# Six inner products in the second matrix product of block 0, with a new home for one set of sums, a shorter layer norm on GpSimd and a remade order table

## The chip, the cores and the metric

The kernel runs on one core of a Trainium2 chip. The metric is the device time of one execution in microseconds. The kernel before takes 338.49 us in the median of three runs (338.16 to 338.64).

In the profile, PE is TensorE's matmuls, PEld its weight loads, DVE is VectorE, ACT is ScalarE, POOL is GpSimd, and SP is SyncE, which issues nearly all transfers (SPq is its sequencer). L868 is line 868 of the kernel's file.

## The reference

```python
def reference(x, w1, b1, w2, b2):      # x (1, 2048, 1024), w1 (1024, 3584), w2 (3584, 1024), all bfloat16
    y = _layernorm(x, axis=-1)         # eps 1e-5
    h = _gelu(jnp.einsum("bsd,df->bsf", y, w1) + b1)
    return jnp.einsum("bsf,fd->bsd", h, w2) + b2
```

## The kernel before

The 2048 rows are worked on in two blocks of 1024. In each block h = gelu(y w1 + b1) comes first, then h w2. Both matrix products use seven products of half-sized operands in place of eight (a Strassen-like scheme). The operands of most of these are sums of quarters of h and w2, made by VectorE, and their results are added up by VectorE and ScalarE.

In the second matrix product, one of the seven products can itself be done by the same scheme. A *plain* product is 4 x 14 matmuls of 512 columns. An *inner* product is 7 half-size products of 14 matmuls of 256 columns, which is an eighth fewer columns, and costs more sums and additions. Which products are inner is a table, with one entry for each block:

```python
SEQ2 = (1, 5, 2, 6, 7, 3, 4)             # the order of the seven products
INNER = ((1, 5, 2, 3, 4), SEQ2)          # block 0: five of them inner; block 1: all seven
```

Block 0 stores its sums of w2 in DRAM, so that block 1 can load them.

All work is a list of operations with dependencies. A planner with estimated durations gives each engine one fixed program, guided by a table of hand-tuned shifts (`ORDER`, some 120 entries). Every engine then gets its program in that order, and an instruction that has to wait holds up all behind it (in a trace below ScalarE stands 5.45 us so, with copies for TensorE behind).

```python
    def _emit(eng, name, ops, sems):   # one engine's program
        for o in ops:
            wait(o.deps)               # semaphores of what it depends on
            inst = o.fn(eng)
            inst.then_inc(sems[o.sem], o.inc)
```

While block 0's second product runs, the rows of block 1 are loaded into eight "x tiles" of 128 rows, normalised, and sent to their transposed place by transposing transfers. The last steps of the layer norm of one tile are:

```python
    vp = add("POOL", 0.2, ... tensor_scalar(out=vpe, in0=sum_of_squares, scalar1=1/D, scalar2=LN_EPS, mult, add))
    rs = add("POOL", 0.6, ... tensor_tensor(out=rstd, in0=vpe, in1=nhalf, op=ALU.pow))      # 1/sqrt
    nb = add("POOL", 0.3, ... tensor_tensor(out=bias, in0=mean, in1=rstd, op=ALU.mult))
    y  = add("ACT", 1.3, ... activation(out=x16, in_=x_sb, func=Identity, scale=rstd, bias=bias))
```

Block 0's product 7 is plain, and product 3 is inner, with its sums of w2 kept in the place of two used w1 tiles (`Y0`):

```python
    M7 = plain(7, S3, B[7], hb, False, [(o,) for o in O12])
    ...                                  # 4 output additions on VectorE, 4 copies O3 on ScalarE
    sub3 = inner(3, S4, inner_sums(3, B[3], Y0, war_of(sub2, 2), True), X0, war_of(sub2), O=..., out=12)
```

Of the kernel before, what the change touches and what calls it, by code (L numbers as in the profile page):

```python
# [23 lines left out]
P = 128  # L24
# [8 lines left out]
INNER = ((1, 5, 2, 3, 4), SEQ2)  # L33
# [6 lines left out]
    G1_5g_0_5:5.5 G1_5g_1_5:8.8 G2_5g_0_3:-15.8 G2_5g_1_3:0.8 G3_5g_0_3:7.3 G3_5g_0_5:-4.7 G3_5g_1_1:-25.3  # L40
    G4_5g_1_1:13 G6_5g_0_5:-21 G7_5g_0_3:9.2 G7_5g_0_5:6.5 M11_1:8.3 M15_0:17 M24_0:-3.1 M27_1:5.7 M43_0:-8.5
    M47_0:7.7 M51_1:7.2 M57_0:16.8 M6_0_0:3.3 M72_1:-20.2 O12_0_1:11.2 O12_0_3:8.4 P1_0_6:10.3 P1_0_9:-1.1
    P1_1_2:-2.7 P1_1_3:-18.7 P1_1_6:0.2 P2_0_12:-1 P2_0_5:0.7 P3_0_10:-9.9 P3_0_11:5.1 P3_0_12:-7.3 P3_0_2:-10.3
    P3_1_6:9.8 P4_0_3:7.4 P4_0_9:-17.7 P4_1_0:40.5 P4_1_1:54.4 P4_1_3:2 P6_0_12:-3.6 P6_0_4:1.1 P6_1_11:4.1
    P7_0_6:-33.7 c7_0_11:2.3 c7_0_5:1.2 c7_0_8:-5.5 c7_0_9:8.4 c7_1_12:9.1 c7_1_13:1.2 g12_1_1:13.1 g12_1_3:2.2
    g21_1_8:25.8 g22_0_2:1.3 g22_0_3:1.6 gS0_5g_1_3:20 gS1_5g_0_3:-6.6 gS1_5g_0_5:11.2 gS3_5g_0_5:14.9 g_0_3_2:-14.6
    hS2_0_1:-7.5 hS3_1_0:8.3 hS4_0_1:-4.8 hS4_0_3:39 iS3_1_1_0:41 iS3_2_0_0:8.3 iS5_3_1_0:28.6 iS5_4_0_0:-14.1
    iS5_5_0_0:-10 iS6_5_0_0:-3.7 iT4_1_0_0:4.1 iT4_2_0_0:3.8 iT4_3_0_0:13.3 iT5_3_0_0:14.2 iT6_1_0_0:4.6
    iT6_2_0_0:1.3 iT6_4_0_0:6.6 iT6_5_0_0:-8.9 k5_3_1:16.7 k5_5g_0_5:35.6 o12_3_0:-17 pT1_2:-34.8 pT1_3:15 pT1_6:4.8
    pT2_1:1.7 pT2_2:7.7 pT3_3:10.8 pT3_5:-2.2 pT4_0:-7.2 pT4_3:-4.3 pT4_4:-7 pT4_5:-2.4 pT4_6:7.9 plain_0_7_2None:35  # L50
    plain_0_7_3None:8.5 pw2_0:-4.4 r11_5g_1_5:-18.2 r12_5_0:10.8 r22_1_0:14.3 r22_5g_0_3:33.7 s2_2_0:-7.2
    sd1_0_2:11.5 sn1_0_9:12.1 sn1_1_10:2.8 sn1_1_5:-0.5 sn5_0_4:-29.1 st0_5_0:-3.9 w1T13_1_0:3.4 w1T1_0_4:30.1
    w1T1_0_6:-5.1 w1T1_1_2:3.5 w1T2_1_1:26.1 w1T3_0_6:-17.7 w1T4_1_3:15 w1_0_0_1:9.9 w1_0_3_0:-7.9 w1_0_5_0:-24
    w1_0_5_1:-0.6 w1_1_0_0:0.7 w1_1_6_1:-1.9 w6_0_11:-4.1 w6_0_5:-9.5 w6_1_5:-44.2 wi5_3:20.8 x0_0_1:-11.2 x1_0:4.8
    y1_6:-8.5 yS1_1_0:6.2 yS2_0_0:8.2 yS2_1_0:-3.4 yS4_1_0:8.6 yi13_1:14.5 yi2_0:-15 yt0_6_0:-2.3
# [5 lines left out]
LAT = 0.12  # L61
PE_LAT = 0.2
# [43 lines left out]
class Planner:  # L106
# [42 lines left out]
    def place(self):  # L149
# [12 lines left out]
        while left:  # L162
# [35 lines left out]
            free[e] = r + c  # L198
# [60 lines left out]
def bass_standalone__mixer_channel_mlp__prompt_kernel(  # L259
# [24 lines left out]
    with ExitStack() as es:  # L284
# [20 lines left out]
        nhalf = sb("nhalf", [P, 1], F32)  # L305
        st_sb = sb("st_sb", [P, NT, 12], F32)
# [75 lines left out]
        c_nh = add("POOL", 0.1, lambda e: e.memset(nhalf[:, :], -0.5), (), -8, "nhalf")  # L382

# [14 lines left out]
        def warm(n, deps, prio):  # L398
# [8 lines left out]
                                                    identity=identb[0:FT, 0:FT]), ())], (c_idb, b1_ld), 11.0, "b1t",  # L407
# [56 lines left out]
        def ln_act2(s, i, prio, war=None):  # L464
# [14 lines left out]
            if junk is junk1:  # L479
                for u in (NU - 2, NU - 1):  # L480
                    h_head.setdefault((22, u), []).append(a2)
            vp = add("POOL", 0.2, lambda e: e.tensor_scalar(out=vpe_sb[:, i:i + 1], in0=st_sb[:, i, 0:1],
                                                           scalar1=1.0 / D, scalar2=LN_EPS, op0=ALU.mult, op1=ALU.add),
                     (a2,), prio + 0.003, f"vpe{s}_{i}")
            rs = add("POOL", 0.6, lambda e: e.tensor_tensor(out=rstd_sb[:, i:i + 1], in0=vpe_sb[:, i:i + 1],
                                                            in1=nhalf[:, :], op=ALU.pow), (vp, c_nh), prio + 0.004,
                     f"rstd{s}_{i}")
            nb = add("POOL", 0.3, lambda e: e.tensor_tensor(out=st_sb[:, i, 1:2], in0=mv_sb[:, i, 1:2],  # L488
                                                            in1=rstd_sb[:, i:i + 1], op=ALU.mult), (rs, a1), prio + 0.005,
                     f"nb{s}_{i}")  # L490
# [82 lines left out]

        def w1_t1(s, c, prio):
            n = s * NC + c
            T1_of[(s, c)] = add("DVE", 0.65, lambda e: e.tensor_tensor(
                out=t1_sb[:, n % 2, 0].rearrange("p k (v c) -> p k v c", v=2), in0=w1raw(n, 0, 1), in1=w1raw(n, 0, 0),
                op=ALU.subtract), [w1_ld[(s, c)][0], *t1_use.get(n - 2, {}).get(1, ())], prio, f"w1T1_{s}_{c}")

        def w1_sums(s, c, prio):  # L580
# [3 lines left out]
            war = t1_use.get(n - 2, {})  # L584

            def tt(k, x0, x1, deps):
                return add("DVE", 0.65, lambda e: e.tensor_tensor(out=tv(k), in0=x0, in1=x1, op=ALU.subtract),  # L587
                           [*deps, *war.get(k, ())], prio + 0.5 * k, f"w1T{k}_{s}_{c}")

            if n > 1 and (s, c) not in GROUPED:  # L590
# [4 lines left out]
                    [*ld, *war.get(1, ()), *war.get(3, ())], prio + 0.5, f"w1T13_{s}_{c}")  # L595
# [5 lines left out]
            w1_use[n] = list(dict.fromkeys((T1, T2, T3, T4)))  # L601
            return {1: T1, 2: T2, 3: T3, 4: T4}
# [3 lines left out]
        def mm1_plain(c, prio):  # L606
# [3 lines left out]
            for b in range(2):  # L610
                hold = [Holder(banks) for _ in range(4)]
                done = {f: [] for f in range(4)}
                for i in range(b * TH, (b + 1) * TH):
                    t = i % TH
                    y = y_in[(0, i)]
                    for j, f in ([(j, f) for j in range(2) for f in range(4)] if i == 0 else
# [7 lines left out]
                        o = add("PE", len(ks) * MM128, fn, list(dict.fromkeys([*done[f][:1]] + [d for _, dd in fn for d in dd])),  # L624
# [244 lines left out]
        x_gate = {}  # L869
        PU = 2  # L870
# [58 lines left out]
        def mm2_block(s, W):  # L929
# [10 lines left out]
            last_ = {}  # L940
            done = lambda p: users[p]
# [94 lines left out]
            def inner(p, a, Yo, xb, war, O=None, bias=None, out=None, gate=(), ogate=(), kk=None, tmp=None, tail=False):  # L1036
# [21 lines left out]
                subs, ev = {}, {}  # L1058

# [284 lines left out]
            for m in (n - 1, n):  # L1344
                w1_use[m] = w1_use[m] + done(3) + kept[3]
# [167 lines left out]
```

## Time and profile before

| | kernel before |
|---|---|
| time, median of 3 | 338.49 us |
| profiled execution | 337.93 us, span 336.2 us |
| TensorE busy | 98% of the span |
| VectorE busy | 84%; 135 to 195 us: 54.6 of 60 us |
| ScalarE, GpSimd busy | 52%, 7% |
| waits of TensorE after its first 8 us | none |

The prediction below shows the lines.

### The profile page before, as it was taken

What the parts mean: (1) busy time and instruction counts of PE and PEld (TensorE: products, weight loads), DVE (VectorE), ACT (ScalarE), POOL (GpSimd) and SP (SyncE); (2) the same over time, 40 slices, a digit from 0 to 9 for tenths busy, and PEclk for the clock granted to TensorE, in tenths of its full rate; (3) what the DMA queues carried; (4) which work ended last, traced back from release to release, by engine and by line L of the source; (5) the groups of instructions that cost most, each with busy time, mean ns of one, the idle gap of its engine ahead of it and who ended that gap; (6) DMA issues with size and microseconds to landing.
All of it is one profiled execution on the core that took longest, in us unless ns stands there. A gap on an engine that the chain in (4) does not pass through costs nothing.

```text
span 336.2 us, 6035 instructions
## 1 busy us (share of the span) xinstructions
PE 329.3 (98%) x2399; PEld 223.3 (66%) x2399; DVE 281.3 (84%) x381; ACT 173.2 (52%) x292; POOL 22.5 (7%) x47
## 2 busy tenths in 40 slices
PE   4999999999999999999999999999999999999996
PEld 4977445445468885547875555544545888888885
DVE  3896789998999999979999888886738879999984
ACT  5675978566786687612113666765676521010200
POOL 2420120000020413200000000000000000000000
PEclk9899999999999999999999999999999999999999
DMA  7896999797868999899859549839971999999103
GB/s 269 257 181 182 355 354 321 247 329 262 279 238 305 353 336 361 227 318 379 320 173 328 181 174 336 288 138 292 351 226 50 386 319 367 333 326 311 65 2 125
DMA packets 80310, 89.47 MB, mean 266 GB/s; under 512 B 15130, under 2 KB 67226, under 8 KB 79770
## 3 DMA queue, kind: packets, MB, share of 16 engines
q1 hardware_dynamic: 80138, 88.95, 81.6%
q8 instruction: 19, 0.31, 0.4%
q10 hardware_dynamic: 144, 0.13, 0.1%
q14 instruction: 9, 0.07, 0.1%
HBM read 61.81 MB, written 24.38 MB: 256 GB/s over the span
## 4 chain that ended last, share of the span: by engine, by line
PE 93%; ACT 3%; POOL 1%; DVE 1%; DMA 1%; issue 0%
PE ps L767 42%; PE ps L1063 34%; PE ps L978 7%; PE ps L619 5%; PE ps L692 5%; DMA x_sb<-in_x_dram 1%; POOL st_sb L488 1%; PE ps L504 1%; ACT t_sb L474 1%; ACT t_sb L469 1%; PE ps L1068 0%; ACT sn_sb L962 0%; ACT ps L962 0%; DVE st_sb L418 0%; ACT x_sb L491 0%
## 5 line engine op out<-in xcount | busy, mean ns | idle before, releaser
L767 PE MATMUL ps<-yw_sb,t_sb 128*128 128x512 f16 x336 | 80.0, 379 | 0.0
L767 PE MATMUL ps<-yw_sb,w_sb 128*128 128x512 f16 x312 | 74.7, 379 | 0.0
L792 ACT ACTIVATE h_sb<-ps,b_sb 128x512 f16<-128x512 f32 x78 | 52.9, 686 | 37.0 <-PE ps L767 32.3
L767 PEld LDWEIGHTS ps<-yw_sb,t_sb 128*128 128x128 f16 x336 | 32.8, 98 | 35.8 <-DVE ps L807 0.2
L767 PEld LDWEIGHTS ps<-yw_sb,w_sb 128*128 128x128 bf16 x312 | 30.3, 98 | 33.2 <-ACT ps L780 0.3
L854 DVE TENSOR_TENSOR h_sb<-h_sb 128x2048 f16<-128x2048 f16 (+2 forms) x36 | 38.6, 1084 | 7.3 <-ACT h_sb L792 5.3
L962 ACT COPY sn_sb<-ps 128x512 f32<-128x512 f32 x27 | 15.5, 583 | 32.9 <-DVE o_sb L942 18.2
L1063 PE MATMUL ps<-w2a_sb,h_sb 128*128 128x256 f16 (+1 forms) x252 | 30.3, 273 | 0.0
L942 DVE TENSOR_TENSOR sn_sb<-ps,sn_sb 128x512 f32<-128x512 f32 x35 | 24.0, 687 | 5.3 <-PE ps L1063 4.6
L1063 PEld LDWEIGHTS ps<-w2a_sb,h_sb 128*128 128x128 f16 x252 | 24.7, 98 | 3.9
L942 DVE TENSOR_TENSOR o_sb<-ps,sn_sb 128x512 bf16<-128x512 f32 (+1 forms) x29 | 19.3, 670 | 6.3 <-PE ps L1063 3.7
L978 PE MATMUL ps<-w2a_sb,h_sb 128*128 128x512 f16 x112 | 24.5, 379 | 0.0
L1063 PE MATMUL ps<-w_sb,t_sb 128*128 128x256 f16 x196 | 23.4, 273 | 0.1
L962 ACT COPY ps<-sn_sb 128x512 f32<-128x512 f32 x12 | 7.1, 589 | 30.3 <-PE ps L1063 24.6
L780 ACT COPY ps<-ps 128x512 f32<-128x512 f32 x26 | 14.9, 577 | 14.6 <-PE ps L767 14.5
L1063 PEld LDWEIGHTS ps<-w_sb,t_sb 128*128 128x128 f16 x196 | 19.0, 98 | 2.7 <-ACT sn_sb L962 0.4
L807 DVE TENSOR_TENSOR ps<-ps,sn_sb 128x512 f32<-128x512 f32 x26 | 17.6, 694 | 3.4 <-PE ps L767 3.3
L792 ACT ACTIVATE h_sb<-sn_sb,b_sb 128x512 f16<-128x512 f32 x26 | 18.5, 717 | 3.7 <-DVE sn_sb L821 2.8
L587 DVE TENSOR_TENSOR t_sb<-w_sb,t_sb 128x1024 f16<-128x1024 bf16 x26 | 17.9, 687 | 2.8 <-PE ps L767 1.6
L978 PEld LDWEIGHTS ps<-w2a_sb,h_sb 128*128 128x128 f16 x112 | 11.0, 98 | 12.8
L821 DVE TENSOR_TENSOR sn_sb<-ps,sn_sb 128x512 f32<-128x512 f32 x20 | 13.6, 686 | 5.1 <-PE ps L767 5.0
L619 PE MATMUL ps<-yw_sb,w_sb 128*128 128x128 f16 x256 | 16.7, 226 | 0.4 <-DVE yw_sb L511 0.4
(125 smaller groups left out, 485.4 us busy)
## 6 DMA issues: line engine op xcount, KB each, us to landing
w_sb<-in_w_dram SPq DMA_DIRECT2D x28, 512.0 KB, 5.6
x_sb<-in_w_dram SPq DMA_DIRECT2D x21, 256.0 KB, 6.0
w_sums<-x_sb SPq DMA_DIRECT2D x21, 256.0 KB, 3.5
w2a_sb<-w_inner_sums SPq DMA_DIRECT2D x12, 448.0 KB, 7.3
x_sb<-in_x_dram SPq DMA_DIRECT2D x15, 256.0 KB, 4.3
w_inner_sums<-w_sb SPq DMA_DIRECT2D x4, 896.0 KB, 8.2
x_sb<-w_sums SPq DMA_DIRECT2D x2, 1792.0 KB, 9.1
w_sb<-w_inner_sums SPq DMA_DIRECT2D x8, 448.0 KB, 6.9
```

The lines of the kernel that those rows point to most:

```text
L587: return add("DVE", 0.65, lambda e: e.tensor_tensor(out=tv(k), in0=x0, in1=x1, op=ALU.subtract), [*deps, *war.get(k, ())], prio + 0.5 * k, ...
L619: fn = [(lambda e, b=b, hb=hold[f], f=f, k=k, t=t: e.matmul(ps[:, hb.k, t * P:(t + 1) * P], lhsT=lhs[:, k, f * P:(f + 1) * P], rhs=yop[f"A ...
L692: fn = [(lambda e, k=k, v=v: e.matmul(ps[:, bank[r].k, v * QN:(v + 1) * QN], lhsT=xo()[:, k, v * P:(v + 1) * P], rhs=yv()[:, k, :], start= ...
L767: fn = [(lambda e, k=k: e.matmul(ps[:, hold[p].k, :], lhsT=lhs[:, k, :], rhs=yop[yo][:, k, :], start=(first and k == 0), stop=(k == KH - 1 ...
L780: return e.copy(out=dst, in_=src) if o_.eng == "ACT" else e.tensor_copy(dst, src)
L792: r = h_ok[(s, q, u)] = add("ACT", 0.70, lambda e: e.activation(out=dst, in_=src(), func=ACT.Gelu_apprx_tanh, bias=b1_sb[:, f:f + 1], scal ...
L807: o2 = add("DVE", 0.7, lambda e: e.tensor_tensor(out=b5v(b5), in0=b5v(b0), in1=v5(), op=ALU.add), (P6, *o5), pt[7] - SLOT, f"w6_{nm}", all ...
L854: o = add("DVE", cost2(w * dst.shape[-1]), lambda e, k0=k0, k1=k1: e.tensor_tensor(out=dst[:, k0:k1, :], in0=a[0][:, k0:k1, :], in1=b[0][: ...
L942: plus = lambda e, out, x, y: e.tensor_tensor(out=out, in0=x, in1=y, op=ALU.add)
L962: return act(lambda e: e.copy(out=out(), in_=src()), deps, at - 5, name, **k)
L978: fn = [(lambda e, k=k, t=t: e.matmul(ps[:, banks_[t].k, :], lhsT=a[0][:, k, t * P:(t + 1) * P], rhs=b[0][:, k, :], start=(first and k == ...
L1063: fn = [(lambda e, k=k, j=j: e.matmul(ps[:, bank[r].k, j * HI:(j + 1) * HI], lhsT=x[0][:, k, j * P:(j + 1) * P], rhs=y[0][:, k, :], start= ...
```

## The change

The intent is to take an eighth of product 7's columns off TensorE, and to find the time and the room for the extra sums elsewhere. The core of the diff, cut (`...` marks cuts):

```diff
-INNER = ((1, 5, 2, 3, 4), SEQ2)
+INNER = ((1, 5, 2, 7, 3, 4), SEQ2)
 ORDER = { ...                       # all entries remade
+OVL = {"DVE": 0.08, "ACT": 0.09}    # the planner lets neighbours on one engine overlap by so much
-            free[e] = r + c
+            free[e] = r + c - OVL.get(e, 0.0)
 ...                                 # layer norm of block 1: one GpSimd step, two new ScalarE steps
-            vp = add("POOL", 0.2, ... tensor_scalar ...
+            vp = add("ACT", 0.2, ... activation(Identity, bias=epsc, scale=1.0 / D) ...
             rs = add("POOL", ... tensor_tensor(... op=ALU.pow) ...
-            nb = add("POOL", 0.3, ... tensor_tensor(... op=ALU.mult) ...
+            nb = add("ACT", 0.2, ... e.mul(...) ...
 ...                                 # block 0: product 7 is inner, its scratch is x tile 7
-            M7 = plain(7, S3, B[7], hb, False, [(o,) for o in O12])
+            gw, okq, sub7 = inner(7, S3, inner_sums(7, B[7], Y0, war_of(sub2, 2)), X0, war_of(sub2),
+                                  O=(gu, ...), kk=x_sb[:, NT - 1, :].bitcast(F32))
+            x_late.append((first_k[7], (NT - 1,)))
 ...                                 # product 3's sums go to x tiles 0 to 6
-            sub3 = inner(3, S4, inner_sums(3, B[3], Y0, war_of(sub2, 2), True), ...
+            Yo3 = inner_sums(3, B[3], [two(xf), *halves(xf)[2:4]], {}, True)
+            x_late.extend((o, range(NT - 1)) for o in users[3])
+            sub3 = inner(3, S4, Yo3, X0, war_of(sub7), ...
 ...                                 # block 1 loads product 7's sums, as block 0 has stored them
-                e7 = t_inner(7, 2, e6 + w1_use[NC + 2], base1[s] + 0.45 * T_MM1)
 ...
+                for o, tiles in x_late:          # wait until these tiles of block 1 are transposed out
+                    o.deps += [d for i in tiles for d in x_free[(s + 1, i)]]
```

## The prediction

> **What bounds the kernel now.** I read first the page's busy shares and the chain that ended last, then the waits of TensorE, then TensorE's timeline, then the busy time of every engine by stage.
>
> ```profile
> PE 329.3 (98%) x2399; PEld 223.3 (66%) x2399; DVE 281.3 (84%) x381; ACT 173.2 (52%) x292; POOL 22.5 (7%) x47
> PE 93%; ACT 3%; POOL 1%; DVE 1%; DMA 1%; issue 0%
> ```
>
> The chain runs through TensorE for 93% of the span. The few per cent on ScalarE and GpSimd in it (108 to 122 us) are a detour of the way back, not a hole: TensorE works through those microseconds too. The waits of TensorE say so plainly, for they are all there are, and all lie in the first 8 us:
>
> ```profile
> PE ps L504 <- DVE x_sb L429: 2.8, 1, 2.8
> PE ps L400 <- POOL ones L375: 1.0, 1, 1.0
> PE ps L619 <- DVE yw_sb L511: 0.4, 1, 0.4
> ```
>
> A busy TensorE need not be at its peak, so I took pitches (start to start) from its timeline:
>
> ```profile
> 134.13 1.69 PE L1063 MATMUL ps<-yw_sb,t_sb 128*128 128x256 bf16 x14
> 135.66 18.29 PE L978 MATMUL ps<-w2a_sb,h_sb 128*128 128x512 f16 x84
> 153.79 1.69 PE L1063 MATMUL ps<-w2a_sb,h_sb 128*128 128x256 bf16 x14
> 155.32 1.69 PE L1063 MATMUL ps<-w_sb,t_sb 128*128 128x256 f16 x14
> ```
>
> 84 matmuls of 512 columns take 153.79 - 135.66 = 18.13 us, 0.2158 us each; 14 of 256 columns take 1.53 us, 0.1092 us each. With these two pitches and 0.0556 us for 128 columns I compared every start in the timeline with where the one before it should end: from 12.6 us to the last matmul (start 331.96 us) the differences add up to about nothing. So the time is 12.6 us of head, then work on TensorE at its pitch without a gap, then 2.7 us of tail from 333.5 to 336.2 us. In such a kernel time falls only with matmul columns, and rises with the first wait that reaches TensorE.
>
> VectorE is the engine that could send such a wait. Busy time by stage, columns PE, PEld, DVE, ACT, POOL:
>
> ```profile
> 95.50:127.00 31.50, 31.38 (x278) 26.85 (x277) 29.20 (x31) 22.66 (x40) 6.85 (x9) 1.00 0.95 315
> 127.00:154.00 27.00, 27.00 (x141) 13.71 (x140) 24.61 (x30) 12.23 (x20) 5.05 (x9) 1.00 1.02 308
> 154.00:175.00 21.00, 21.00 (x187) 18.06 (x185) 20.06 (x23) 3.92 (x7) 0.00 (x0) 1.00 0.75 282
> 175.00:190.00 15.00, 15.00 (x87) 8.25 (x85) 13.61 (x23) 5.80 (x10) 0.00 (x0) 1.00 0.72 214
> 190.00:257.00 67.00, 67.00 (x349) 33.87 (x347) 48.27 (x68) 44.08 (x73) 0.00 (x0) 1.00 0.73 246
> ```
>
> 95.5 to 175 us is the second matrix product of block 0, which the change rewrites. VectorE is busy there 73.9 of 79.5 us. Its back-to-back instructions overlap by some 0.08 us (a 1.08 us sum starts every 1.00 us), so by pitches the demand is 28.3 + 24.5 + 19.0 = 71.8 us and the true slack 7.7 us. From 175 to 190 us the slack is 1.5 us, from 190 to 257 us it is 22.6 us, and from 60 to 95.5 us 3.0 us.
>
> **What the Trainium skill says.** "TensorE: Matmul & The Clock Gate", section "Wait — 56ns, not 53.3ns?", gives N / 2.4 GHz + 2.5 ns from start to start for a warm array: 215.8 ns at 512 columns, 109.2 ns at 256. The trace agrees (215.8 and 109.2 ns). A column thus costs about the same in both shapes, and fewer columns is fewer microseconds. "VectorE: DVE Perf Modes", section "The perf-mode tier table (the rule you actually need)", has a two-tensor operation at 2x for 16-bit data in SBUF (1224 ns at 2048 elements) and at 1x with an operand in PSUM. The trace agrees: 1217 ns for 128x2048 f16, 688 ns for a 128x512 addition from PSUM. So the 512-element additions that empty banks are dear. "SBUF — State Buffer", section "Who interferes with whom", says that a VectorE instruction with two SBUF inputs contends with a GpSimd instruction that reads SBUF. The same GpSimd multiplication of 128x1 takes 0.19 us at 122.43 us and 2.82 us at 113.97 us of the trace, which fits that, though no run here isolates it.
>
> **The change part by part.**
>
> 1. Product 7 of block 0 turns from 4 x 14 = 56 plain matmuls of 512 columns into 7 half-size products of 14 matmuls of 256 columns, 98 in all. Removed: 56 x 0.2158 = 12.09 us. Added: 98 x 0.1092 = 10.70 us. On the path: -1.39 us. This is the only term that is certain to lie on the path.
>
> 2. VectorE's share in block 0. Added: four operand sums of h (1.00 us pitch each, 4.0); the sums of w2 for product 7, one of 3584 elements and two of 1792 (1.93 + 1.0 + 1.0 = 3.9); six evictions or additions from PSUM (0.60 pitch each, 3.6); two output additions of 1024 f32 (1.225 us, pitch 1.14, 2.3). Removed: four output additions (4 x 0.60 = 2.4). Net +11.4 us. On the path only as far as it doesn't fit; see the first rival.
>
> 3. In block 1 the load of product 7's w2 operand, its sums (2.02 + 1.09 + 1.09 us, pitch 3.9) and their stores go, because block 0 now stores them. They sit at about 212 to 227 us, where VectorE has slack and TensorE never waited: 0 on the path.
>
> 4. ScalarE: four copies U for the four O3, so about equal, two more copies for product 7 (1.2 us), and two 0.2 us steps per tile of the layer norm of block 1 taken from GpSimd (8 x 0.4 = 3.2 us). It is busy 3.92 of 21 us in the late stage: 0 on the path.
>
> 5. GpSimd's three steps (means 0.37, 0.57, 0.90 us, with two more hand-overs) become one between two ScalarE steps. A tile of x is normalised some 1.3 us earlier, and those with a blocked multiplication 2 to 3 us. No TensorE wait ends there now. It serves part 6.
>
> 6. Product 3's sums of w2 move into x tiles 0 to 6, and product 7 uses tile 7 as scratch, so both wait until block 1's tiles have been transposed out. The last transposes are issued at 143.4 to 147.1 us and land 5.0 us later by the median, near 150 us. Product 3 will start near 141.7 + 10.7 = 152.4 us and needs its first sum one half-product (1.53 us) later. That is a margin of 2 to 3 us, widened by part 5: 0 expected. Tile 7 is normalised early; its transpose waits on product 2 (ends 135.66 us), some 7 us before the scratch is wanted.
>
> 7. The order table and the planner's overlap term move nothing by themselves. They decide how well 2 is hidden. In the head (6.84 to 12.6 us) about 2.1 us go to a slow clock (the first 16 matmuls take 1.9 us instead of 0.9) and short waits; the new order may gain or lose some 0.3 us there. I count 0.
>
> Sum without a new wait: -1.39 us, 338.49 - 1.39 = 337.1 us.
>
> **The rivals.**
>
> *VectorE becomes the bound in block 0.* Demand 71.8 + 11.4 = 83.2 us against 79.5 - 1.4 = 78.1 us: 5.1 us don't fit in the stage. Before it 3.0 us are idle and after it 1.5 us up to 190 us, so even perfect packing leaves about 0.6 us to be done after 190 us, where there is plenty of room. Speaking for it: the slack is a set of small waits for TensorE's results, which never vanish altogether, and at the start of block 1 TensorE needs the sums of y and w1 (about 7 us of VectorE) before it can go beyond the first two units' two free products (3.45 us). Speaking against: the sums can run ahead of need by several microseconds, stores can lag, and an order table remade for just this with the overlap counted should move them. If a third of the 5.1 us reaches TensorE, the gain is gone (338.8 us); if all of it, about 342 us.
>
> *The x tiles come free too late.* If the last transpose lands 2 us after need, VectorE stands in line at product 3's first sum while being short of time already: +1 to +2 us, 338 to 339 us. The transposes took up to 4.05 us to issue and 11.7 us to land at worst, which speaks for it; the shorter layer norm against.
>
> *The gain is hidden anyway.* With another bound underneath, fewer columns would buy nothing: 338.5 us. TensorE's three waits, all before 8 us, speak against it.
>
> **Range and chances.** The two cases of a clean schedule (337.1) and of 0 to 1.5 us of new waits I hold about equally likely, since someone has remade the order around exactly this bottleneck. The middle is 337.4 us. Low: clean, with 0.3 us from the head and 0.3 us of run-to-run spread (338.16 to 338.64 before), 336.5 us. High: waits that eat the gain, 338.8 us. 2% is 6.8 us: faster by that is out of reach, as only 1.39 us of columns go; slower would take all the surplus of VectorE on the path and more.
>
> **What would show it.** Right: 56 fewer 512-column and 98 more 256-column matmuls; still no wait of TensorE after 13 us, VectorE at over 95% from 95 to 175 us, and less idle after 190 us used up. Wrong: matmuls waiting on VectorE's sums of y, w1, h or w2 near 141 to 185 us (first rival), or VectorE idle for a transpose or for x near 143 to 155 us (second); a head longer than 12.6 us would spoil the sum from another side.

## The result, and the profile after

The changed kernel took 340.00 us in the median (four runs: 341.18, 340.18, 339.73, 339.83). The kernel before took 338.33 us in the same rounds. The ratio is 1.0055 with a 95% interval of 1.0030 to 1.0081. A ratio is always the mean time of one kernel's runs over the mean of the other's runs of the same rounds, so it isn't quite the ratio of the medians. Executions over 1.5% slower than the fastest of the same kernel are left out of the means. The changed kernel is slower by some 1.8 us, within 2%, and outside my range of 336.5 to 338.8 us.

The profiled execution is the slowest of the four, 341.18 us (span 339.4). Its busy shares and its chain that ended last, as two lines of the page:

```profile
PE 330.5 (97%) x2441; PEld 227.9 (67%) x2441; DVE 286.3 (84%) x389; ACT 177.0 (52%) x310; POOL 19.9 (6%) x32
PE 86%; DMA 4%; ACT 3%; SPq 2%; issue 2%; POOLq 2%; POOL 0%; DVE 0%; ACTq 0%
```

There are 42 more matmuls, as 98 - 56 demands, and 15 fewer GpSimd instructions. The chain lost 7 points on TensorE. The waits of TensorE say where (line, tile, releaser; then us in total, how often, longest):

```profile
PE ps L513 <- DVE x_sb L439: 2.3, 1, 2.3
PE ps L1081 <- ACT ps L979: 2.1, 1, 2.1
...
PE ps L781 <- DMA w_sb<-in_w_dram: 0.3, 1, 0.3
```

The first is the old wait of the head. The second is new and lies in product 7: TensorE waits for a ScalarE copy. The third is a w1 load of block 1 that comes late. The timeline around the second shows what ScalarE was doing. Columns are start, duration, engine and line, operation, output<-inputs, count, and in brackets the idle time before it with its releaser:

```profile
137.15 1.08 DVE L868 TENSOR_TENSOR t_sb<-h_sb 128x1792 f16<-128x1792 f16 x1
137.22 0.28 ACT L492 ACTIVATE vpe_sb<-st_sb,epsc 128x1 f32<-128x1 f32 x1
137.58 5.34 POOL L495 TENSOR_TENSOR rstd_sb<-vpe_sb,nhalf 128x1 f32<-128x1 f32 x1 [4.07 <-ACT vpe_sb L492]
...
140.16 2.35 DVE L868 TENSOR_TENSOR h_sb<-h_sb 128x2048 f16<-128x2048 f16 x2
...
142.95 0.29 ACT L498 ACTIVATE st_sb<-mv_sb,rstd_sb 128x1 f32<-128x1 f32 x1 [5.45 <-POOL rstd_sb L495]
143.28 1.24 ACT L500 ACTIVATE x_sb<-x_sb,st_sb,rstd_sb 128x1024 f16<-128x1024 bf16 x1
144.42 1.80 ACT L979 COPY sn_sb<-ps 128x512 f32<-128x512 f32 x3
145.09 1.89 DVE L959 TENSOR_TENSOR sn_sb<-ps,sn_sb 128x512 f32<-128x512 f32 x3 [2.58 <-ACT sn_sb L979]
146.12 0.60 ACT L979 COPY ps<-sn_sb 128x512 f32<-128x512 f32 x1
```

GpSimd's only step, for x tile 5, took 5.34 us on 128 numbers. VectorE ran five sums with two SBUF inputs (SBUF is on-chip memory) back to back from 137.15 to 142.51 us, and the step ended 0.4 us after that run did. ScalarE stood in line for it with nothing else to do in its program, then did the two steps of the layer norm, and only at 144.42 us came to product 7's copies: three that copy results out of the banks in which TensorE sums them (`ps`), then at 146.12 us one that puts an earlier sum into a bank. TensorE starts 0.05 us after this one ends. Its own timeline shows the price:

```profile
142.96 1.69 PE L1081 MATMUL ps<-w_sb,t_sb 128*128 128x256 f16 x14
146.77 2.73 PE L1081 MATMUL ps<-w2a_sb,h_sb 128*128 128x256 f16 x14 [2.12 <-ACT ps L979]
149.29 2.37 PE L1081 MATMUL ps<-w_sb,t_sb 128*128 128x256 f16 x14
151.50 1.69 PE L1081 MATMUL ps<-w2a_sb,t_sb 128*128 128x256 f16 x14
```

At the full pitch 14 matmuls take 1.53 us. From 142.96 to 146.77 us is 3.81 us, so 2.28 us are lost. The next 14 take 2.52 us and the 14 after them 2.21 us, because the clock is slow after the pause (granted clock 0.6 from 146.77 to 151 us): another 0.99 + 0.68. Together that's 3.95 us. With 0.3 us for the w1 load and -1.39 us for the columns the sum is 2.9 us, and this run lies 341.18 - 338.33 = 2.85 us above the kernel before. Without the slow clock this run would have taken 341.18 - 1.67 = 339.5 us, close to where the other three lie (339.73 to 340.18). They have no trace, so that they had the same wait at the full clock is an inference, not shown.

A second trace of the very same kernel (the run l_changed_again, profiled at 339.2 us) has GpSimd's step at 0.55 us and no wait there:

```profile
138.50 0.29 ACT L498 ACTIVATE st_sb<-mv_sb,rstd_sb 128x1 f32<-128x1 f32 x1 [0.66 <-POOL rstd_sb L495]
```

The two traces differ in when the step begins: 0.43 us after VectorE's first sum has begun in the first trace, 0.18 us before it in the second. So whether this wait strikes is a matter of tenths of a microsecond, and in this sense luck. The waits of TensorE in the second trace that are not in the head:

```profile
PE ps L1081 <- DVE x_sb L868: 0.7, 1, 0.7
PE ps L1081 <- ACT ps L794: 0.4, 1, 0.4
...
PE ps L1081 <- DMA w2a_sb<-in_w_dram: 0.2, 1, 0.2
```

All three lie between 152 and 161 us, in product 3, and with what they delay they cost 0.41 + 0.87 + 0.56 = 1.84 us. In order of time:

```profile
154.41 1.69 PE L1081 MATMUL ps<-w2a_sb,h_sb 128*128 128x256 bf16 x14 [0.24 <-DMA w2a_sb<-in_w_dram]
156.81 1.70 PE L1081 MATMUL ps<-x_sb,t_sb 128*128 128x256 f16 x14 [0.72 <-DVE x_sb L868]
160.64 1.69 PE L1081 MATMUL ps<-x_sb,t_sb 128*128 128x256 f16 x14 [0.40 <-ACT ps L794]
```

With the columns that gives 1.84 - 1.39 = 0.45 us; the run lies 339.20 - 338.57 = 0.63 us above the kernel before of its rounds. VectorE's and SyncE's timelines of that run show why (SyncE's second column is the time that issuing took):

```profile
153.02 1.23 DVE L959 TENSOR_TENSOR o_sb<-sn_sb 128x1024 bf16<-128x1024 f32 x1
155.66 1.09 DVE L868 TENSOR_TENSOR x_sb<-w2a_sb 128x1792 f16<-128x1792 bf16 x1 [1.42 <-DMA yw_sb<-x_sb]
...
140.18 5.10 SPq L529 DMA_TRANSPOSE yw_sb<-x_sb  x3
145.32 1.19 SPq L359 DMA_DIRECT2D w2a_sb<-in_w_dram  x2
146.56 3.44 SPq L529 DMA_TRANSPOSE yw_sb<-x_sb  x2
```

VectorE is idle for 1.42 us before product 3's first sum, until the last transpose out of tile 5 has landed. That transpose was issued by 150.0 us and landed at about 155.6 us. The queue on SyncE was busy with transposes and loads back to back, so it couldn't go earlier in this order. In the kernel before the last transposes went earlier (`143.41 3.68 SPq L520 DMA_TRANSPOSE yw_sb<-x_sb  x2`), and nothing of product 3 waited for them. So there are two hold-ups, one in front of the other: when the first strikes, everything behind it is late anyway and the second doesn't show (the first trace has no wait for product 3's sums).

### The profile page after: what moved, and what is told of

Its sections match the earlier page's. It is cut to its first block, busy times and chain, and to the rows that moved or that the text cites.

```text
span 339.4 us, 6125 instructions
## 1 busy us (share of the span) xinstructions
PE 330.5 (97%) x2441; PEld 227.9 (67%) x2441; DVE 286.3 (84%) x389; ACT 177.0 (52%) x310; POOL 19.9 (6%) x32
## 4 chain that ended last, share of the span: by engine, by line
PE 86%; DMA 4%; ACT 3%; SPq 2%; issue 2%; POOLq 2%; POOL 0%; DVE 0%; ACTq 0%
PE ps L1081 39%; PE ps L781 37%; PE ps L706 4%; DMA w_sb<-in_w_dram 4%; PE ps L633 4%; SPq L359 2%; POOLq L292 2%; ACT t_sb L484 1%; ACT x_sb L500 1%; ACT t_sb L479 1%; PE ps L513 1%; ACT sn_sb L979 0%; PE ps L1086 0%; POOL rstd_sb L495 0%; ACT ps L979 0%
## 5 line engine op out<-in xcount | busy, mean ns | idle before, releaser
L781 PE MATMUL ps<-yw_sb,t_sb 128*128 128x512 f16 x336 | 80.5, 379 | 0.0
L781 PE MATMUL ps<-yw_sb,w_sb 128*128 128x512 f16 x312 | 76.0, 379 | 0.3 <-DMA w_sb<-in_w_dram 0.3
L781 PEld LDWEIGHTS ps<-yw_sb,t_sb 128*128 128x128 f16 x336 | 32.6, 98 | 36.0 <-DVE t_sb L605 0.5
L781 PEld LDWEIGHTS ps<-yw_sb,w_sb 128*128 128x128 bf16 x312 | 30.2, 98 | 32.8 <-DMA w_sb<-in_w_dram 0.8
L868 DVE TENSOR_TENSOR h_sb<-h_sb 128x2048 f16<-128x2048 f16 (+2 forms) x36 | 38.4, 1085 | 1.5 <-PE ps L1081 1.4
L1081 PE MATMUL ps<-w2a_sb,h_sb 128*128 128x256 f16 (+1 forms) x280 | 34.5, 278 | 2.1 <-ACT ps L979 2.1
L959 DVE TENSOR_TENSOR sn_sb<-ps,sn_sb 128x512 f32<-128x512 f32 x40 | 27.0, 685 | 6.8 <-PE ps L1081 4.1
L1081 PEld LDWEIGHTS ps<-w2a_sb,h_sb 128*128 128x128 f16 x280 | 27.7, 99 | 6.8 <-ACT ps L979 2.4
L979 ACT COPY sn_sb<-ps 128x512 f32<-128x512 f32 x27 | 15.6, 583 | 29.9 <-PE ps L1081 16.5
L979 ACT COPY ps<-sn_sb 128x512 f32<-128x512 f32 x13 | 7.6, 589 | 37.2 <-PE ps L1081 37.1
L1081 PE MATMUL ps<-w_sb,t_sb 128*128 128x256 f16 x196 | 24.0, 277 | 0.0
L1081 PEld LDWEIGHTS ps<-w_sb,t_sb 128*128 128x128 f16 x196 | 19.6, 100 | 3.0
L959 DVE TENSOR_TENSOR o_sb<-ps,sn_sb 128x512 bf16<-128x512 f32 (+1 forms) x25 | 16.6, 666 | 5.1 <-PE ps L1081 3.2
L868 DVE TENSOR_TENSOR t_sb<-h_sb 128x1792 f16<-128x1792 f16 x16 | 17.4, 1086 | 1.5 <-PE ps L781 1.3
L495 POOL TENSOR_TENSOR rstd_sb<-vpe_sb,nhalf 128x1 f32<-128x1 f32 x8 | 11.8, 1479 | 109.8 <-ACT vpe_sb L492 109.8
L633 PE MATMUL ps<-yw_sb,w_sb 128*128 128x128 f16 x256 | 17.4, 229 | 0.6 <-DVE yw_sb L520 0.4
L633 PEld LDWEIGHTS ps<-yw_sb,w_sb 128*128 128x128 bf16 x256 | 16.0, 103 | 1.7 <-DMA w_sb<-in_w_dram 1.0
```

The source lines that it names most:

```text
L495: rs = add("POOL", 2.0, lambda e: e.tensor_tensor(out=rstd_sb[:, i:i + 1], in0=vpe_sb[:, i:i + 1], in1=nhalf[:, :], op=ALU.pow), (vp, c_nh ...
L633: fn = [(lambda e, b=b, hb=hold[f], f=f, k=k, t=t: e.matmul(ps[:, hb.k, t * P:(t + 1) * P], lhsT=lhs[:, k, f * P:(f + 1) * P], rhs=yop[f"A ...
L781: fn = [(lambda e, k=k: e.matmul(ps[:, hold[p].k, :], lhsT=lhs[:, k, :], rhs=yop[yo][:, k, :], start=(first and k == 0), stop=(k == KH - 1 ...
L868: o = add("DVE", cost2(w * dst.shape[-1]), lambda e, k0=k0, k1=k1: e.tensor_tensor(out=dst[:, k0:k1, :], in0=a[0][:, k0:k1, :], in1=b[0][: ...
L959: plus = lambda e, out, x, y: e.tensor_tensor(out=out, in0=x, in1=y, op=ALU.add)
L979: return act(lambda e: e.copy(out=out(), in_=src()), deps, at - 5, name, **k)
```

## The experiments

The theory after reading these traces had two parts. *First hold-up*: ScalarE's program has the layer norm of tile 5 ahead of product 7's copies, and GpSimd's step in it can be held for microseconds by VectorE. *Second hold-up*: the x tiles as home make product 3 wait for tile 5's transposes. The rivals were my prediction's first one, that VectorE is simply full, and that the remade order loses time in other places.

In the edits, `behind(queue, x, mark)` takes the operation x out of one engine's program and puts it right behind `mark`. Such an edit keeps the dependencies, so that waits follow the operations. From f_home_undone on (l_changed_again excepted), the kernels replay the changed kernel's programs from a record, so that an edit moves nothing else. The record makes their files longer: the changed kernel's lines L495, L781, L868, L959, L979 and L1081 are L656, L942, L1029, L1120, L1140 and L1242 there. Every run gave correct results. Runs that were sent together (a, b, d, e; f, g, h; j, k, l; m, n; o, p; q, r, s; t) shared a chip and the runs of before.

### First group: the layer norm

**a_copies_first.** ScalarE's last two layer norm steps of tile 5 go behind product 7's copies.

```diff
+        behind("ACT", "nb1_5", "k1_7_0")
+        behind("ACT", "y1_5", "nb1_5")
```

> Edit: the changed kernel, with the last two ScalarE steps of tile 5's layer norm (its bias and its normalisation) put behind the five copies that stand after them in ScalarE's queue; nothing else moved. Theory Q (the queue): the 2.1 us wait of TensorE at 146.8 us comes from those copies standing behind a layer-norm step that waits for GpSimd, whose one step took 5.34 us while VectorE ran sums from SBUF back to back. Then the wait and the slow clock after it vanish and the time is 338.4 - 1.4 + 0.3 to 0.9 for the small gaps at 183 to 242 us: 337.3 to 338.0 us, ratio 0.997 to 0.999. Rival V (VectorE has 5 us too much to do between 95 and 190 us): the wait only moves to another place, 339.5 to 340.3 us. Rival X (x tiles free too late): tile 5 is now transposed some 2 us later, product 3's first sum waits, 340.5 us or more.

It measured 338.99 us against 338.96 before, ratio 1.0005 (0.9981 to 1.0028). So some 1.5 us come back by the ratios, short of the 0.997 to 0.999 that I expected. The wait in product 7 is gone from the trace, the waits in product 3 are all there, and VectorE idles 1.60 us for the transposes. In this one trace GpSimd's step took 0.55 us, so that it doesn't test the order under stress; r_tiles_and_copies does (and h_loads_first, where the step took 5.34 us too).

**b_three_pool_steps.** The three GpSimd steps of before in the changed kernel's order.

```diff
+        # vpe1_i (tensor_scalar) and nb1_i (tensor_tensor mult) go back to POOL, around rstd1_i
+        order["POOL"][k:k + 1] = [v, order["POOL"][k], m]
```

> Edit: the changed kernel with the three GpSimd steps per tile of the kernel before (variance plus eps, power, bias) instead of one between two ScalarE steps; every other instruction in its place. Theory Q: ScalarE now waits at the normalisation itself, for a chain of three steps of which any can be held up; the wait of TensorE near 146 us stays and grows by up to 1 us: 340 to 342 us, ratio 1.005 to 1.011. Rival S (the two added ScalarE steps are what delays ScalarE): back to 338 us or below. Rival V: as the changed kernel, 340 us.

It measured 340.34 us, ratio 1.0038 (1.0013 to 1.0062): within the noise of the changed kernel, and below the 1.005 to 1.011 that I expected. GpSimd's steps took up to 3.89 us here, but those of tile 5 were not held in this trace (0.19 to 0.55 us). The way back to three steps cures nothing that these runs can tell.

**d_vector_spacer.** Four VectorE instructions on one element each, amid the run of sums, to let GpSimd in.

```diff
+        for j in range(4):      # behind iT6_7_0_0 in VectorE's program
+            o = Op("DVE", 0.1, lambda e, j=j: e.tensor_scalar(out=scr[:, j:j + 1], in0=mv_sb[:, 0, 1:2], ...
```

> Edit: the changed kernel with four added VectorE instructions of one element per partition with one SBUF input (about 0.1 us each, results unused) in the middle of the run of five sums from SBUF during which GpSimd's step for tile 5 took 5.34 us. Theory Q with the hold-up by VectorE's two-input SBUF sums: GpSimd's step gets in at the spacer and takes under 2.5 us, ScalarE's wait shrinks from 5.45 to under 2.5 us, TensorE's wait near 146 us falls to 0 to 0.4 us, and more VectorE work makes the kernel faster: 337.3 to 338.4 us, ratio 0.997 to 1.000. Rival V: 0.4 us more VectorE work in the fullest stage, 340.1 to 340.6 us. If GpSimd's step is long for another reason (its own start-up): 340 us, step still above 5 us.

It measured 339.66 us, ratio 1.0022 (0.9996 to 1.0048). In its trace GpSimd's step began at 137.88 us and took 2.07 us: it ended 0.2 us after the spacers (139.45 to 139.78 us), not after the whole run of sums. This fits the picture that it's VectorE's unbroken run that holds GpSimd. ScalarE's wait (2.18 us) and TensorE (none near 146 us) did as expected; the time did not. The step also takes 0.55 us in traces without a spacer, so one trace doesn't prove it. A count over the 17 traces with the changed kernel's order (the edits apart) that are not slow says more:

| tile 5's GpSimd step began | traces | took | ended |
|---|---|---|---|
| 0.05 to 0.80 us before the run of five sums | l, a, b, f, m, q | 0.55 us | |
| 0.03 to 0.43 us after the run's begin | g, j, k, o, s | 1.06 to 1.46 us | 0.41 us after the first sum's end |
| 0.42 to 0.43 us after it | the changed kernel, h, p, r | 5.34 us | 0.41 us after the last sum's end |
| 0.43 us after it, spacers | d | 2.07 us | 0.42 us after the second sum's end |
| within an earlier sum with two SBUF inputs | t | 1.20 us | 0.40 us after that sum's end |

So a step that starts inside such a sum always ended 0.4 us after the end of one. Which one it is, the first of the run or the last, isn't explained by these runs: the step of k began as late as that of the changed kernel, and got in behind the first.

**e_norm_alone.** The kernel before with nothing but the layer norm changed.

```diff
-            vp, nb on POOL
+            vp = ACT activation(Identity, bias=epsc, scale=1/D);  nb = ACT mul
```

> Edit: the kernel before with part 5 alone: layer norm of block 1 with one GpSimd step between two ScalarE steps, every other instruction in its place. Theory Q: there the copies behind the layer norm have slack, so 338.2 to 338.7 us, ratio 0.999 to 1.001, no wait of TensorE after 13 us. Rival N (the new form of the layer norm is itself the loss): 339.5 us or more. If shortening the chain helps by itself: below 338 us.

It measured 338.24 us, ratio 0.9982 (0.9956 to 1.0008), with no wait of TensorE after the head. The layer norm's new form harms nothing by itself. With b, which kept the new order and lost about as much, that points to the order.

### Second group: the home of product 3's sums

**f_home_undone.** Product 3's sums go to the old place again, the two w1 tiles, which product 7's sums now use just before. The loads of two later w1 tiles move behind product 3's stores, as the place demands; all runs up to p keep this.

```diff
-            Yo3 = inner_sums(3, B[3], [two(xf), *halves(xf)[2:4]], {}, True)
-            x_late.extend((o, range(NT - 1)) for o in users[3])
+            Yo3 = inner_sums(3, B[3], Y0, war_of(sub7, 7), True)
```

> Edit: the changed kernel with product 3's inner sums of w2 put back into the w1 slots (home of product 7's sums, freed by product 7's half-products) instead of the x tiles, so that they no longer wait for the transposes out of x; the loads of w1 chunks 1 and 2 of block 1 moved behind product 3's stores, as the slots need; all else in its place. Theory of two waits (first: ScalarE's copies behind GpSimd's step near 146 us, 0 to 3.7 us, luck of the run; second: product 3's operands near 153 to 161 us, 1.3 to 2.3 us whenever the first is absent): the second is taken away except for the late load of product 3's raw w2 (0.3 to 0.4 us); the first stays where it strikes. 338.3 to 340.5 us, ratio 1.000 to 1.005; no wait of TensorE for x_sb sums. Rival V (VectorE over-full): no change, ratio 1.004 to 1.006.

**g_home_and_copies** is f with the edit of a.

> Edit: f_home_undone and a_copies_first together. Two waits: both gone but for the late raw load of product 3's w2 (0.3 to 0.9 us) and the small ones after 180 us (0.3 to 0.8 us): ratio 0.997 to 0.9995. If the second wait were the load of raw w2 alone and not the home: as a_copies_first, ratio 1.000 to 1.001. Rival V: ratio 1.003 or more.

**h_loads_first** is g with product 3's raw w2 loads ahead of the last transposes, and the two halves of w1's last tile loaded together.

```diff
+        behind("SP", "w2_0_B22_1", "is7_0")
+        behind("SP", "w2_0_B22_0", "is7_0")
+        behind("SP", "w1_1_6_0", "w1_1_6_1")
```

> Edit: g_home_and_copies, and in the queue of DMA issues the two loads of product 3's raw w2 ahead of the three transposes that stood before them, and the last w1 half of block 1 ahead of the first loads for the last products. Two waits: TensorE has no wait between 13 us and the end over 0.2 us; all of the 1.39 us is kept: ratio 0.995 to 0.997, faster than the kernel before by 1.0 to 1.7 us. Rival V: ratio above 1.000 with waits on VectorE between 141 and 185 us.

They measured 343.16, 344.01 and 344.14 us: ratios 1.0127 (1.0091 to 1.0162), 1.0155 (1.0123 to 1.0188) and 1.0161 (1.0139 to 1.0184). All are slower than the changed kernel, and all three expectations were missed. In h TensorE runs from 146 to 158 us without a gap, so neither hold-up is there, though GpSimd's step took 5.34 us in it. But a third wait takes their place, 4.5 us of TensorE at 164.59 us (3.5 and 3.4 us in f and g). VectorE's timeline of h names its cause:

```profile
161.22 1.09 DVE L1029 TENSOR_TENSOR w_sb<-w2a_sb,w_sb 128x1792 f16<-128x1792 bf16 x1 [4.67 <-DMA w_inner_sums<-w_sb]
```

Product 3's sum waits for the store of product 7's sum from the same place, as that store is issued late. In this order the x tiles thus spare VectorE a wait of 4.7 us at the price of one of 1.4 us. That the home was moved for this reason is likely.

### Third group: undoing that wait, and VectorE's room

**i_vector_doubled** was a first try at doubling VectorE sums. One doubled sum had no wait on its copy, a race. It ran nowhere.

> Edit: h_loads_first with three of VectorE's sums (1.0 us each, in products 7 and 3 of block 0) done twice, 3 us more VectorE work in the fullest stretch. Rival V says VectorE has no room there: 2 to 3 us longer than h_loads_first. The theory of two waits says the order left room by moving VectorE work into the first product of block 1: 0 to 1 us longer than h_loads_first.

**j_store_early** is h with the store of product 7's third sum issued early.

```diff
+        behind("SP", "is7_2", "is7_0")
```

> Edit: h_loads_first, and the store of product 7's third sum moved up in the queue of DMA issues, directly behind the store of its first two. In h_loads_first VectorE stood 4.67 us at product 3's third sum for that store, because with the home put back the sum overwrites what the store reads; TensorE stood 4.5 us at 164.6 us for it. Theory: this was the only wait left; the store now lands near 147 us, before product 3 needs the place, and TensorE runs from 13 us to the end with gaps of 0.3 us in all: ratio 0.995 to 0.998. Rival V (VectorE over-full between 95 and 190 us): other waits on VectorE of 2 us or more stay: ratio 1.003 or more.

It measured 340.23 us, ratio 1.0050 (1.0029 to 1.0071). TensorE's first wait is now at 169 us, 2.05 us, for the next such store (VectorE stands 2.63 us for it). One wait goes and the next in line comes up.

**k_vector_doubled** is j with three of VectorE's sums done twice.

```diff
+        for name in ("iS3_7_0_0", "iT4_7_0_0", "iS5_3_0_0"):   # in VectorE's program
+            # the same sum once more, just before itself
```

> Edit: j_store_early with three of VectorE's sums (1.0 us each, in products 7 and 3 of block 0) done twice, 3 us more VectorE work in the fullest stretch. Rival V says VectorE has no room there: 2 to 3 us longer than j_store_early. If the new order left room by moving VectorE work into the first product of block 1: 0 to 1 us longer.

It measured 340.99 us, ratio 1.0065 (1.0047 to 1.0084), only 0.8 us above j. But TensorE waited 2.2 us for VectorE near 156 us, and its next 28 matmuls took 1.7 us too long at a slow clock, while the wait of 2.05 us for the store was gone. The one hides the other, so this doesn't settle VectorE's room.

**l_changed_again** is the changed kernel once more, unedited.

> The changed kernel itself once more, for a second trace beside the same chip's runs of the kernel before. Theory of two waits: ratio 1.003 to 1.008 again; in the trace either ScalarE's copies behind GpSimd's step near 146 us (TensorE loses 1 to 4 us there) and little after it, or, if that step gets in at once, waits near 153 to 161 us for product 3's sums in the x tiles and its raw w2, 1.3 to 2.4 us in all. Rival V: the same 1.5 to 2 us with VectorE never idle between 141 and 185 us.

It measured 339.72 us (339.20 to 341.76), ratio 1.0047 (1.0021 to 1.0073), which confirms the result. Its trace is the second one shown above.

**m_stores_early** is j with the fourth sum's store early too; **n_doubled_again** is m with the doubled sums of k.

```diff
+        behind("SP", "is7_3", "yt1_5_0")
```

> Edit: j_store_early, and the store of product 7's fourth sum moved up too, ahead of the last transpose of tile 5 and of 2.8 MB of loads. In j_store_early TensorE ran without a gap through products 7 and 3 until 169 us, where VectorE's last sum of product 3 stood 2.63 us for that store and TensorE 2.0 us behind it. Theory: with it TensorE has no wait over 0.4 us after its head, and the 1.39 us of columns are kept: ratio 0.995 to 0.998. If another wait comes up in its place: 1.000 to 1.005.

> Edit: m_stores_early with the same three VectorE sums done twice as in k_vector_doubled (3 us more). There TensorE lost 4 us near 156 us to VectorE while the store's wait at 169 us went, 0.8 us longer in sum, so the two covered each other. Rival V in its weaker form (VectorE just fits and has no room): here nothing is covered, 2.5 to 4 us longer than m_stores_early. If VectorE had room: 0 to 1 us longer.

m measured 338.95 us against 338.65, ratio 1.0009 (0.9983 to 1.0035). After the head a single wait of TensorE is left, 1.5 us at 158.11 us for the first w1 tile of block 1, whose load now stands behind five transposes in SyncE's queue. n's runs gave a ratio of 1.0054 (1.0027 to 1.0080), some 1.5 us above m; its profiled run (498.64 us, clock 0.66) is not used. That's between what the two theories expected, since the wait for w1 could cover a part.

### Fourth group: the last wait

**o_w1_before_transposes** is m with that w1 load ahead of tile 5's transposes; **p_doubled_no_w1_wait** is o with the doubled sums.

```diff
+        behind("SP", "w1_1_0_1", "yt1_4_1")
+        behind("SP", "w1_1_0_0", "yt1_4_1")
```

> m_stores_early with the two loads of w1_1_0 issued ahead of tile 5's transposes. If the 1.39 us of columns are to be had once every operand of product 3 and the first w1 tile come in time: no wait of TensorE after the head, time 1.0 to 1.6 us below before (ratio 0.995 to 0.997). If VectorE has no room (my prediction's first rival): the 1.5 us wait for w1 goes, but waits on VectorE's sums of about the same size appear within 155 to 190 us, ratio 0.999 to 1.002. If tile 5's transposes, now later by the loads' issue, hold product 3's first sum again: VectorE idle for yw_sb near 155 us and a wait of 0.5 to 1 us there, ratio 0.998 to 1.001.

> o_w1_before_transposes with three VectorE sums done twice (about 4 us more of VectorE work between 140 and 170 us), no wait of TensorE left to cover it. If VectorE is close to the bound there: 2.5 to 4 us above o. If it has room: 0 to 1 us above o. n_doubled_again, where a wait for w1 could cover part, was some 1.5 us above its pair.

o measured 337.48 us (336.99 to 338.90) against 338.48, ratio 0.9968 (0.9942 to 0.9994). It beats the kernel before by 1.1 us, and by the ratios the changed kernel by 2.7 to 2.9 us. Its busy time by stage, columns as in the prediction:

```profile
135.00:150.00 15.00, 15.00 (x103) 9.92 (x102) 14.81 (x17) 8.10 (x16) 1.41 (x2) 1.00 1.15 310
150.00:165.00 15.00, 15.00 (x124) 11.79 (x122) 14.96 (x19) 2.23 (x4) 0.00 (x0) 1.00 1.19 320
165.00:180.00 15.00, 15.00 (x132) 12.68 (x131) 14.86 (x18) 1.68 (x3) 0.00 (x0) 1.00 1.02 364
180.00:195.00 15.00, 14.99 (x75) 6.94 (x73) 14.76 (x23) 9.54 (x16) 0.00 (x0) 1.00 0.71 236
```

TensorE is busy all 60 us and VectorE 59.4 of them (54.6 before). Both are full at once, so the work fits, and nothing more does. p shows that: 341.14 us, ratio 1.0084 (1.0057 to 1.0112), 3.7 us above o for 3.0 us more VectorE work (289.4 against 286.4 us busy). Its trace has TensorE wait for VectorE:

```profile
155.95 1.70 PE L1242 MATMUL ps<-w_sb,h_sb 128*128 128x256 f16 x14 [2.22 <-DVE sn_sb L1120]
```

So VectorE has next to no room there, but in the changed kernel's two traces it isn't what TensorE waits for first.

### Fifth group: the x tiles kept

**q_waits_by_tile.** The changed kernel in its own home, but each of product 3's four sums waits only for the tiles that it overwrites. The home covers 7168 elements, and the first sum writes the first 1792 of them, which is tiles 0 and 1, not tile 5.

```diff
-            x_late.extend((o, range(NT - 1)) for o in users[3])
+            x_late.extend(zip(users[3], ((0, 1), (3, 4, 5), (1, 2, 3), (5, 6)), strict=True))
```

> The changed kernel and its order, but each of product 3's four sums waits for the x tiles that it overwrites (0-1, 3-5, 1-3, 5-6) and no longer for all of 0 to 6. If the second wait is the landing of tile 5's transposes, which the first sum doesn't overwrite: VectorE no longer idle about 1.5 us for yw_sb at 155 us, TensorE's wait of 0.7 us on that sum gone or halved, ratio 0.9995 to 1.002 (1 us below the changed kernel), with the wait behind GpSimd's step still there in some runs. If it is VectorE's room or the raw w2 load that holds product 3: no change, ratio 1.004 to 1.0055.

It measured 339.91 us against 338.69, ratio 1.0028 (1.0007 to 1.0048), so some 0.8 us better than the changed kernel's 1.0055 and 1.0047. The intervals overlap, so the time alone doesn't show a gain, and it's a little short of the 1.002 that I had expected at most. But the trace is plain. VectorE goes straight into the sum that had stood 1.42 us:

```profile
154.12 1.23 DVE L1120 TENSOR_TENSOR o_sb<-sn_sb 128x1024 bf16<-128x1024 f32 x1
155.26 1.08 DVE L1029 TENSOR_TENSOR x_sb<-w2a_sb 128x1792 f16<-128x1792 bf16 x1
```

TensorE's wait for it is gone. The wait for the raw w2 load, 0.2 us in l, is 0.7 us here, so part of the gain was only moved.

**r_tiles_and_copies** is q with the edit of a. **s_w2_loads_from_scalar** is r with the two raw w2 loads of product 3 issued by ScalarE.

> q and a_copies_first together: both causes that I name taken away, with the x tiles' home kept. If these two are all: ratio 0.997 to 0.999 (only the 0.4 us wait for raw w2 is left of TensorE's waits), no run of the slower form. If VectorE has no room: about 1.000, like a_copies_first.

> r with product 3's two raw w2 loads issued by ScalarE (idle there) instead of SyncE, ahead of the copies' end at about 145 us, so that SyncE reaches tile 5's transposes 1.2 us earlier. If the queue on SyncE is what makes product 3's operands late: the 0.4 us wait for w2a goes too, ratio 0.996 to 0.998. If the transfers themselves are slow (DMA share over 1 there): the landing doesn't move, ratio as r.

r measured 338.39 us, ratio 0.9999 (0.9979 to 1.0018), 1.7 us better than the changed kernel and yet short of what I expected. Its trace is the best test of the first hold-up, for GpSimd's step was held for 5.34 us again:

```profile
139.90 5.34 POOL L656 TENSOR_TENSOR rstd_sb<-vpe_sb,nhalf 128x1 f32<-128x1 f32 x1 [4.07 <-ACT vpe_sb L653]
...
145.28 1.69 PE L1242 MATMUL ps<-w_sb,t_sb 128*128 128x256 f16 x14
146.81 1.69 PE L1242 MATMUL ps<-w2a_sb,h_sb 128*128 128x256 f16 x14
```

TensorE took no notice, because the copies now stand ahead of the held layer norm steps. In r TensorE has no gap over 0.2 us from 42.3 to 240 us. What is lost lies outside: a head longer by some 0.8 us, 0.3 us for a w1 load at 240 us, and a wait at 42 us. VectorE's and TensorE's lines of r for that one:

```profile
39.12 0.69 DVE L751 TENSOR_TENSOR t_sb<-w_sb 128x1024 f16<-128x1024 bf16 x1 [1.47 <-DMA w_sb<-in_w_dram]
...
42.27 1.90 PE L942 MATMUL ps<-yw_sb,t_sb 128*128 128x512 f16 x8 [0.76 <-DVE sn_sb L960]
```

The remade order has this sum of w1 *ahead* of two additions that empty TensorE's banks; the kernel before has it behind them. When the w1 load is late, the additions are late with it. It strikes in some traces only (not in the changed kernel's two).

s measured 338.43 us, ratio 1.0014 (0.9982 to 1.0047). Four of its six runs lie at 337.8 to 338.7 us and two at 340.7 us, and its profiled run has no wait for raw w2. The interval spans both expectations, so s is inconclusive; why two of its runs are slow stays open, as they have no trace.

**t_and_two_w1_places** is r with the two places of the order set back.

```diff
+        behind("SP", "w1_1_6_0", "w1_1_6_1")
+        behind("DVE", "w1T1_0_3", "c7_0_3")
+        behind("DVE", "w1T2_0_3", "w1T1_0_3")
```

> r_tiles_and_copies with two places of the remade order set back: the sums of w1 for tile 3 behind the two evictions at 38 to 41 us (as before has them), and the first half of w1's last tile loaded right behind its second half. If the rest of the lost time in r is the remade order's own short waits for w1 (0.8 us at 42 us where the load came late, 0.3 us at 240 us): TensorE gap-free from 13 us to its last matmul, time 0.5 to 1.2 us below r, ratio 0.996 to 0.998. If it is the head or run-to-run spread: as r, 0.999 to 1.001.

It measured 337.90 us against 338.72, ratio 0.9978 (0.9960 to 0.9996), 0.7 us better than r, though on another chip and with overlapping intervals. It, too, beats the kernel before, by 0.7 us, with the change's own home kept, and the changed kernel by more. Six of its seven runs lie at 337.4 to 338.3 us. The profiled one is the seventh, 341.09 us: its head has a 1.2 us wait for w1, and there are two waits of 0.7 us (VectorE's sum) and 0.6 us (raw w2) in products 7 and 3, so a gap-free TensorE in the other six is likely but not shown.

## Why the prediction was wrong

Class and direction: "within 2%" was right; the time of 340.0 us lies 1.2 us above my range, and the sum has the wrong sign.

- **Step 1, the columns (-1.39 us): right.** The pitches are the same and the counts are as worked out. The gain is real: o and t show 1.1 and 0.7 us of it once the waits are gone (both intervals end just below 1), so the third rival (hidden anyway) falls.
- **Step 2 and the first rival, VectorE: the size right, the verdict half right.** The durations of VectorE's instructions (count times mean, over all groups of the trace) add up to 308.5 us against 300.3 us before; my terms give 11.4 - 3.9 = 7.5 us more. VectorE does get full (59.4 of 60 us in o), and p shows that 3 us more would cost 3.7 us. I held it likely that some of the surplus would reach TensorE. It fits when the operands come in time, as more work moves than I thought: from 190 to 257 us VectorE is busy 48.6 us in o, where before less the 3.9 us of step 3 leaves 44.4, so by estimate some 4 us went past 190 us and not 0.6. The full VectorE is also the likely reason why each small wait of it goes straight to TensorE, as there is little slack to make it up.
- **Step 4, ScalarE "0 on the path": wrong.** I counted ScalarE's busy time (3.92 of 21 us) and not its program order. It was idle most of the time while it held TensorE up, because a step that waited for GpSimd stood ahead of the copies. r and h show that the order is the cause: with the copies ahead, a step of the same 5.34 us costs nothing.
- **Step 5, "no TensorE wait ends there now": true of before only.** In before, ScalarE waited for GpSimd up to 2.25 us, without harm. I had read the GpSimd instruction of 2.82 us and named the contention. What I missed is that the new order puts it into the chain to TensorE, beside a run of five sums on VectorE with which it took 5.34 us. e shows that the new form alone is harmless.
- **Step 6, the x tiles ("a margin of 2 to 3 us ... 0 expected"): wrong.** Tile 5's transpose was issued by 150.0 us, against at most 147.1 us in before, and landed not 5.0 but 5.6 us later. So its tile was free at 155.6 us, where I had put 150. Without waits TensorE would have taken the first sum at 152.47 + 2 x 1.53 = 155.5 us, later than the 153.9 us that I had put, and VectorE had to start it 1.1 us before that. The margin was -1.2 us. My second rival priced this at +1 to +2 us; the measured loss in l is 1.84 us with the raw load's part. What I had not seen is that it wasn't needed: the first sum waits for a tile that it doesn't touch (q).
- **Step 7, the order table ("0.3 us"): probably mis-sized.** By the ratios t gives back 0.7 us from two places of the remade order; the head's own spread comes on top, and the intervals of r and t overlap.

The sum thus reads: -1.39 us of columns, and about 3.1 us of waits to get to +1.7 us. By the ratios a and q together give back 1.7 us (r against the changed kernel), and the two w1 places 0.7 us (t against r). How the 1.7 us divide between the two hold-ups is open: the other runs of the changed kernel have no trace. The remaining 0.7 us to -1.39 us are not settled. The heads of the traces differ from run to run by about as much.

## What to carry to other kernels

In a kernel with one engine full, look at the order of the other engines' programs and not at their busy shares: an engine that's half idle still stops the full one when an instruction that waits stands ahead of one that frees or fills a buffer. When memory changes hands, let each writer wait for what it overwrites and not for the whole region. And when a wait is taken away, look for the next in line before you judge the change: here three came up one after the other (4.5, 2.0 and 1.5 us). Take more than one trace of a kernel, too: two of this one showed two different waits.

## What the Trainium skill lacked or had wrong

- "SBUF — State Buffer", section "Who interferes with whom", has it that a VectorE instruction with two SBUF inputs contends with a GpSimd instruction that reads SBUF; the traces agree: in all eleven in which tile 5's step on 128x1 began inside such an instruction, it ended 0.40 to 0.42 us after the end of one. It doesn't say how long a run of such instructions back to back can keep GpSimd out: of ten that began in the first of five sums, five got in behind it (1.06 to 1.46 us), four only behind the last (5.34 us), and one behind the second (2.07 us, one-element instructions came next). Begun before the run, the step took 0.55 us.
- "TensorE: Matmul & The Clock Gate", section "Part 1: The HAM clock gate", puts the slow clock after an idle window of about 3.4 us. Here a wait of 2.12 us was enough: the next 14 matmuls of 256 columns took 2.52 us, where 1.53 us is the full pitch. It isn't certain either: after a wait of 2.22 us they took 2.02 us in k and 1.54 us in p, and after 2.05 us in j 1.52 us.
- "Advanced Engine Details and Errata", section "X-Bar Transpose (TRN2)", has it that "TRN2 transpose DMAs are as fast as regular DMAs" and gives a bandwidth, but no time for issuing one, and no page has it for this shape on trn2 (a table on trn3 has cycles for "previous generations"). In the trace of l the transposing transfers of 128x512 2-byte elements shown above held SyncE's queue for 1.7 us each (5.10 for three, 3.44 for two), where the two plain loads between them took 0.6 us each (a plain store at 152.10 us took 1.98 us, so the kind isn't all). Here it's this queue that made tile 5 late.
